# Fewer and larger DMAs, a third tile for f, and a newly searched order in an attention and FFN kernel

## The chip, the cores and the metric

The kernel runs on one core of one Trainium2 chip. The metric is the device time of one execution in microseconds (us), the median over runs; lower is better. The core has TensorE (PE in the profile, with its weight loads PEld), VectorE (DVE), ScalarE (ACT), GpSimd (POOL) and SyncE (SP), which here issues every DMA.

## The reference

Attention over 4 batches, 8 heads, 576 positions of 64 elements, with a retrieval from a memory mixed in by a gate; its output, laid out as 2304 tokens of 512, goes through a feed-forward network (FFN) of width 2048. Cut to what is computed:

```python
scores = scale * q @ k.T                      # causal: -1e9 above the diagonal
a = exp(scores - scores.max(-1)); a /= a.sum(-1) + 1e-9
local = a @ v
phi = lambda x: where(x > 0, x, exp(x) - 1.0) + 1.0
mem_out = (phi(q) @ M_prev) / ((phi(q) @ z_prev) + 1e-6)
g = sigmoid(beta)                             # one per head
attn = g * mem_out + (1 - g) * local          # 4 x 8 x 576 x 64
x = attn.transpose(0, 2, 1, 3).reshape(2304, 512)
h = x @ w_in                                  # 512 x 2048
out = (h * tanh(softplus(h))) @ w_out         # 2048 x 512
```

The weights w_in and w_out come as 64-bit floating point numbers; the kernel reads them as pairs of 32-bit words.

## The kernel before, in words

**Attention** goes by 16 pairs of heads, p = 4 bb + c for batch bb and quarter c of d_model; the text counts them from pair 1 (p = 0). `pair(p)` loads `f` (q and k transposed, 576 KB in all, in two DMAs, in four for pair 1), `qn` (q by rows), `z` (the memory's normaliser, one DMA per pair, spread over the partitions) and `v`. Then come S, the scores into PSUM banks (`bank<-f`); on DVE the mask with the running maximum (`w<-bank,mask`); on ACT the exponential with its sum (`w<-w,mx`); on GpSimd mostly the division by the sum (`w<-w,rc`); T, transposes into banks (`bank<-ident,w`), which ACT and DVE copy to `at`; and V, the product with v and the memory (`bank<-at,v`). Its result x is split in two parts: ACT copies the rounded part to `xo` (`CAST xo<-bank`), DVE puts the rest in `xl`. Both parts go by DMA to DRAM (`xs`), and for the first 512 tokens straight to the FFN's tile `xg` as well.

**FFN.** The 2048 hidden units are 16 units of 128. The first KA = 4 units run while attention goes, in five blocks of up to 512 tokens (`early`): `slot_h` makes h (`bank<-xg,wt`, three matmuls for each of four quarters, since x and the weights each are in two parts), ACT applies the activation and `out_a` multiplies by w_out (`bank<-wt,xg`); `ob` takes the sums to DRAM. The first block (block 0) takes x from pairs 1 to 4. The other 12 units follow after attention, in two groups of six: for each group three blocks of 768 tokens (a *round* each), in which `factors` loads x from `xs` and forms seven factors, `products` makes a two-by-two block product with seven products in place of eight (`bank<-xT,wi`, 126 matmuls a round), and `outputs` multiplies by w_out (`bank<-wt,xg`, 108 matmuls a round).

**Weights.** `word` loads one unit's words into `raw` (512 KB) and turns them into 32-bit numbers in five steps: ACT scales the high words (`ca<-raw`), DVE takes the sign and joins it, ACT scales the low words (`cs<-raw`), POOL adds both (`ca<-ca,cs`). `halves` then splits the number in two parts in `wt` or, by `split7`, in `wi`. ACT must load another function table to go from the exponential to the FFN's activation and back.

**What sets the order.** `Plan` is a list scheduler that runs when the program is built. Every operation has an engine, an estimated length, a priority (smaller goes first) and the buffers that it holds; a buffer is a tile of a `Ring` of fixed size, and an operation may be placed only when its ring has a free tile. `pick` chooses for each engine the ready operation of the best priority, `place` books its time, `schedule` repeats this until all are placed. On the chip each engine executes its list in that order and waits where an operand is not there. A priority in attention is `T0[p] + OFF[step]`: T0 is a number for each pair, OFF one for each kind of step ('lf' the load of f, 'lv' of v, 'S' the scores, 'V', and so on); CV gives the priority of the early units' conversions, and the numbers FB, FS, XP and TB those of the FFN. For TensorE the rule in `pick` prefers attention when it is ready and changes between attention and FFN by DRAIN, AGE and STAY. TABLE is what a change of ACT's table counts. EA = 6 is the number of pairs whose `nrm` scalings and phi step go partly by ACT. A transfer is planned at 370 GB/s, one behind the other on one wire, with 1.4 us behind it:

```python
if o.eng == "SP":
    self.wire = max(self.wire, start + 0.9) + o.kb / 370.0
    done = self.wire + 1.4
```

The rings that matter here: f 2 tiles, z 2, v 2, `xo` 2, `xl` 1, `raw` 2, `ca` 3, `cs` 3, `ob` 4. The tiles of attention are in one pool that is given back ahead of the first operation of the tail (`tail_tiles`).

## Time and profile before

| what | value |
|---|---|
| median of three runs | 569.87 us (568.3 to 571.32) |
| profiled execution: its time | 567.94 us |
| profiled execution: its span | 566.1 us |
| TensorE busy | 532.8 us, 94% of the span |
| VectorE busy | 433.6 us, 77% |
| ScalarE busy | 343.3 us, 61% |
| GpSimd busy | 192.0 us, 34% |
| moved by DMA | 99.78 MB, mean 176 GB/s |
| mean granted TensorE clock | 0.979 |

The span is the time from the first to the last recorded instruction; the execution's time adds 1.84 us around it. Shares of the whole span are means over stages that have different limits, so the rows below go by stage: the busy time of each engine in a stretch, and the timelines, in which a bracket at the end of a row is the time that the engine was idle ahead of it and what it had waited for. Since every instruction goes through one helper (`Queue`), all rows have that helper's line, L260, and are told apart by the tiles: `bank<-f` is a score, `bank<-at,v` is V, `bank<-xg,wt` makes h. The page's groups of TensorE leave out the tail's difference between early and late units: `bank<-wt,xg` is used by both.

### The profile page before, as it was taken

What the parts mean: (1) busy time and instruction counts of PE and PEld (TensorE: products, weight loads), DVE (VectorE), ACT (ScalarE), POOL (GpSimd) and SP (SyncE); (2) the same over time, 40 slices, a digit from 0 to 9 for tenths busy, and PEclk for the clock granted to TensorE, in tenths of its full rate; (3) what the DMA queues carried; (4) which work ended last, traced back from release to release, by engine and by line L of the source; (5) the groups of instructions that cost most, each with busy time, mean ns of one, the idle gap of its engine ahead of it and who ended that gap; (6) DMA issues with size and microseconds to landing.
All of it is one profiled execution on the core that took longest, in us unless ns stands there. A gap on an engine that the chain in (4) does not pass through costs nothing.

```text
span 566.1 us, 10611 instructions
## 1 busy us (share of the span) xinstructions
PE 532.8 (94%) x3684; PEld 442.2 (78%) x3684; DVE 433.6 (77%) x1039; ACT 343.3 (61%) x812; POOL 192.0 (34%) x268
## 2 busy tenths in 40 slices
PE   5596969999999999999999999999999899999997
PEld 3474647777776777788988899899889788989985
DVE  5799886999977985269779959749969995773722
ACT  6799889997999976366577235137328631521510
POOL 2578664798693797001121500000012310000000
PEclk9788979999999999999999999999999999999999
DMA  7566754676657742796556555444475617624004
GB/s 243 172 232 229 242 182 149 207 219 214 221 177 218 242 117 65 237 337 199 185 191 239 178 175 168 129 150 156 142 227 167 222 38 223 185 68 157 0 7 143
DMA packets 60740, 99.78 MB, mean 176 GB/s; under 512 B 6928, under 2 KB 32016, under 8 KB 60688
## 3 DMA queue, kind: packets, MB, share of 16 engines
q1 hardware_dynamic: 60688, 99.12, 54.2%
q8 instruction: 29, 0.48, 0.4%
q14 instruction: 23, 0.19, 0.1%
HBM read 73.40 MB, written 23.59 MB: 171 GB/s over the span
## 4 chain that ended last, share of the span: by engine, by line
PE 57%; DVE 16%; DMA 12%; ACT 9%; issue 3%; SPq 2%; POOL 1%; ACTq 0%; DVEq 0%
PE bank L260 57%; DMA raw<-in_w_out_dram 4%; DVE w L260 4%; ACT w L260 2%; SPq L260 2%; DMA part<-ob 2%; DVE at L260 2%; ACT L260 1%; DVE ca L260 1%; DMA f<-in_f_src_dram 1%; DMA qn<-in_qn_dram 1%; DVE xt L260 1%; DMA ob<-part 1%; DMA raw<-in_w_in_dram 1%; DVE wt L260 1%
## 5 line engine op out<-in xcount | busy, mean ns | idle before, releaser
L260 PE MATMUL bank<-wt,xg 128*128 128x512 f32 x864 | 200.9, 391 | 2.4 <-ACT wt L260 1.8
L260 PEld LDWEIGHTS bank<-wt,xg 128*128 128x128 f32 x864 | 161.2, 188 | 37.8 <-ACT wt L260 2.1
L260 PE MATMUL bank<-xT,wi 128*128 128x384 f32 x756 | 134.1, 335 | 1.9 <-DVE xg L260 1.1
L260 PEld LDWEIGHTS bank<-xT,wi 128*128 128x128 f32 x756 | 131.3, 188 | 3.8 <-DVE xg L260 2.1
L260 POOL TENSOR_TENSOR ca<-ca,cs 128x512 int32<-128x512 int32 x32 | 50.7, 1592 | 200.2 <-ACT cs L260 200.2
L260 ACT ACTIVATE w<-w,mx 128x576 f32<-128x576 f32 (+4 forms) x160 | 88.4, 558 | 9.4 <-DVE mx L260 9.1
L260 POOL TENSOR_SCALAR w<-w,rc 128x192 f32<-128x192 f32 (+4 forms) x148 | 85.4, 597 | 11.4 <-DVE rc L260 7.1
L260 ACT ACTIVATE bank<-bank 128x384 f32<-128x384 f32 (+2 forms) x92 | 45.2, 495 | 64.8 <-DVE bank L260 54.6
L260 DVE CUSTOM_DVE_ANT_0 w<-bank,mask 128x288 f32<-128x288 f32 (+4 forms) x160 | 60.3, 423 | 14.2 <-PE bank L260 14.2
L260 PE MATMUL bank<-f 64*128 64x288 f32 (+4 forms) x384 | 60.2, 442 | 10.4 <-DMA f<-in_f_src_dram 10.0
L260 PE MATMUL bank<-at,v 128*64 128x256 f32 (+2 forms) x512 | 57.4, 378 | 4.6 <-ACT at L260 3.7
L260 PE MATMUL bank<-xg,wt 128*128 128x512 f32 (+1 forms) x240 | 55.6, 382 | 6.1 <-DMA xg<-xl 2.7
L260 PEld LDWEIGHTS bank<-f 64*128 64x128 f32 x384 | 39.7, 204 | 26.4 <-issue 14.8
L260 DVE TENSOR_TENSOR xg<-bank,xg 128x384 fp32r<-128x384 f32 (+2 forms) x92 | 50.5, 567 | 12.0 <-ACT xg L260 11.8
L260 PEld LDWEIGHTS bank<-at,v 128*64 128x64 f32 x512 | 37.4, 143 | 25.1 <-ACT at L260 5.9
L260 PEld LDWEIGHTS bank<-xg,wt 128*128 128x128 f32 x240 | 41.5, 191 | 16.4 <-DMA xg<-xl 3.3
L260 DVE TENSOR_TENSOR ob<-bank,ob 128x512 f32<-128x512 f32 x36 | 24.4, 686 | 38.6 <-PE bank L260 36.3
L260 ACT CAST xg<-bank 128x384 fp32r<-128x384 f32 (+2 forms) x92 | 44.2, 501 | 0.9
L260 DVE COPY at<-bank 128x448 f32<-128x448 f32 x64 | 39.0, 646 | 5.3 <-PE bank L260 5.2
L260 PEld LDWEIGHTS bank<-ident,w 64*128 64x128 f32 x928 | 34.1, 142 | 10.2 <-issue 7.3
L260 DVE TENSOR_TENSOR bank<-u,bank 128x384 f32<-128x384 f32 x72 | 38.2, 556 | 3.7 <-PE bank L260 3.5
L260 PE MATMUL bank<-ident,w 64*128 64x64 f32 x928 | 37.1, 228 | 4.1 <-DVE ca L260 1.9
(53 smaller groups left out, 552.1 us busy)
## 6 DMA issues: line engine op xcount, KB each, us to landing
part<-ob SPq DMA_DIRECT2D x36, 256.0 KB, 3.1
xT<-xs SPq DMA_DIRECT2D x24, 384.0 KB, 6.3
ob<-part SPq DMA_DIRECT2D x36, 256.0 KB, 3.4
f<-in_f_src_dram SPq DMA_DIRECT2D x30, 288.0 KB, 4.5
raw<-in_w_in_dram SPq DMA_DIRECT2D x16, 512.0 KB, 5.0
raw<-in_w_out_dram SPq DMA_DIRECT2D x16, 512.0 KB, 4.4
qn<-in_qn_dram SPq DMA_DIRECT2D x16, 320.0 KB, 4.6
v<-in_vn_dram SPq DMA_DIRECT2D x16, 320.0 KB, 3.4
```

Source lines behind the costliest of these rows:

```text
L260: ins = f(*a, **kw)
```

## The change

- **DMAs.** f of a pair comes in one DMA instead of two (pair 1 keeps four). z comes for four pairs at once, into one tile `zall` that all pairs read; its ring is gone. The two parts of x lie side by side in one tile `xo` of [128, 2S], and leave in one DMA each to `xs` and, for the first 512 tokens, to `xg`. The tail's x factors are loaded per quarter with both parts in one, where it was per part with both quarters. The program has 306 DMAs in place of 361.
- **The planner's count of DMAs.** `place` keeps the planned ends of all transfers, and a DMA is planned no earlier than the end of the eighth one back (LANES = 8).
- **Rings.** f has three tiles. While attention runs, `ca` has one tile (was three), `cs` two (three), `ob` three (four); when attention's pool is given back, MORE adds `ca` 2, `cs` 1 and `ob` 1.
- **Numbers of the order.** T0, OFF, CV, DRAIN, AGE, STAY, TABLE (6 to 25.5), FS (20 to 8.7) have other values, and the tail's priorities have values of their own in TP. EA is 5. The planner's lengths of TensorE's operations grow by 0.05 to 0.06, and up to 90 us (COLD) they count 1.16 fold (before: 1.2 fold up to the first FFN matmul).

The core of the diff:

```diff
-EA = 6
+EA = 5
-CV = (21.0, 34.0, 41.0, 48.0)
-T0 = tuple(10.0 * p for p in range(16))
+CV = (32.0, 37.5, 46.3, 57.5)
+T0 = (0.0, 8.0, 25.7, 28.8, 41.7, 50.6, 62.1, 80.5, 89.4, 103.7, 106.9, 113.6, 118.4, 128.0, 130.0, 143.1)
...
-SLOTS = {"f": 2, "qn": 2, "phe": 1, "z": 2, "v": 2, "w": 6, "at": 6, "xo": 2, "xl": 1, "mx": 4, "sm": 2, "den": 3,
-         "rc": 2, "ob": 4, "raw": 2, "ca": 3, "cs": 3}
-KEPT = ("ob", "raw", "ca", "cs")
+SLOTS = {"f": 3, "qn": 2, "phe": 1, "v": 2, "w": 6, "at": 6, "xo": 2, "mx": 4, "sm": 2, "den": 3, "rc": 2}
+KEPT = {"raw": 2, "ca": 1, "cs": 2, "ob": 3}
+MORE = {"ca": 2, "cs": 1, "ob": 1}
+LANES = 8
...
         if o.eng == "SP":
             self.wire = max(self.wire, start + 0.9) + o.kb / 370.0
             done = self.wire + 1.4
+            self.landed.append(done)
+            self.lane = self.landed[-LANES] if len(self.landed) >= LANES else 0.0
...
-            s = max(now, o.ready, t, self.port if o.port else 0.0)
+            s = max(now, o.ready, t, self.port if o.port else 0.0, self.lane if eng == "SP" else 0.0)
...
-        chunks = [(0, 288), (S + 448, 2 * S), (288, S), (S, S + 448)] if p == 0 else [(0, S), (S, 2 * S)]
+        chunks = [(0, 288), (S + 448, 2 * S), (288, S), (S, S + 448)] if p == 0 else [(0, 2 * S)]
...
-        P.op("SP", 0.4, lambda: sy.dma_start(out=at(zb), in_=zz[:, 2 * p:2 * p + 2, :].rearrange("a b c -> a (b c)").to_broadcast([128, 2 * D])),
-             t0 + OFF['lq'] + 1.0, w=[k("z")], bufs=[zb], kb=64)
+        if c == 0:
+            z0 = slice(2 * D * p, 2 * D * p + 8 * D)
+            P.op("SP", 0.4, lambda: sy.dma_start(out=zall[:, z0], in_=zz[:, 2 * p:2 * p + 8, :].rearrange("a b c -> a (b c)").to_broadcast([128, 8 * D])),
+                 t0 + OFF['lz'], w=[("z", bb)], kb=400)
...
-        P.op("SP", 0.4, lambda: sy.dma_start(out=xs[bb][:, 0, c, :], in_=at(xob)), t0 + 5, r=[k("xo", 0), k("xo", 1)], w=[("xs", bb, c, 0)], bufs=[xob], kb=288)
-        P.op("SP", 0.4, lambda: sy.dma_start(out=xs[bb][:, 1, c, :], in_=at(xlb)), t0 + 5, r=[k("xl", 0), k("xl", 1)], w=[("xs", bb, c, 1)], bufs=[xlb], kb=288)
+        P.op("SP", 0.4, lambda: sy.dma_start(out=xs[bb][:, :, c, :], in_=at(xb2).rearrange("p (i t) -> p i t", i=2)), t0 + 5,
+             r=done, w=[("xs", bb, c, i) for i in range(2)], bufs=[xb2], kb=576)
...
-            split7(q, TB - 20 + 300 * gi + 5 * q)
+            split7(q, TB + TP['wi'] + TP['gap'] * gi + 5 * q)
```

What the numbers do to the order is seen in the lists of instructions themselves. SP at the program's start, before:

```order
L260 DMA f_101<-in_f_src_dram 128x288
L260 DMA f_101<-in_f_src_dram 128x128
L260 DMA f_101<-in_f_src_dram 128x288
L260 DMA f_101<-in_f_src_dram 128x448
L260 DMA f_102<-in_f_src_dram 128x576 x2
L260 DMA qn_103<-in_qn_dram 128x640
L260 DMA z_106<-in_zz_dram 128x128
L260 DMA qn_104<-in_qn_dram 128x640
L260 DMA z_107<-in_zz_dram 128x128
L260 DMA gt<-in_beta_dram 128x8
L260 DMA v_108<-in_vn_dram 128x640
L260 DMA v_109<-in_vn_dram 128x640
```

and after:

```order
L272 DMA v_104<-in_vn_dram 128x640
L272 DMA f_98<-in_f_src_dram 128x288
L272 DMA f_98<-in_f_src_dram 128x128
L272 DMA f_98<-in_f_src_dram 128x288
L272 DMA f_98<-in_f_src_dram 128x448
L272 DMA v_105<-in_vn_dram 128x640
L272 DMA f_99<-in_f_src_dram 128x1152
L272 DMA qn_101<-in_qn_dram 128x640
L272 DMA zall<-in_zz_dram 128x512
L272 DMA gt<-in_beta_dram 128x8
L272 DMA qn_102<-in_qn_dram 128x640
L272 DMA f_100<-in_f_src_dram 128x1152
```

v of pairs 1 and 2 now stand ahead of their f, z comes once, and f of pair 3 (`f_100`) is the twelfth DMA.

TensorE from the end of pair 4's V on, before (`xg` is x of block 0, `wt_81` and `wt_82` the first two units' w_in, `f_101` the scores of a later pair):

```order
L260 MATMUL bank_70<-at_120,v_109 64x128
L260 MATMUL bank_73<-xg,wt_82 128x512 x9
L260 MATMUL bank_74<-f_101 128x288
L260 MATMUL bank_75<-f_101 128x288
L260 MATMUL bank_70<-f_101 128x288
L260 MATMUL bank_71<-f_101 128x288
L260 MATMUL bank_76<-xg,wt_81 128x512 x3
L260 MATMUL bank_72<-f_101 128x448
L260 MATMUL bank_77<-f_101 128x448
L260 MATMUL bank_72<-f_101 128x64
L260 MATMUL bank_77<-f_101 128x64
L260 MATMUL bank_74<-f_101 128x320
```

and after, from the middle of the scores of pair 7 on, which follow pair 4's V:

```order
L272 MATMUL bank_76<-f_98 128x448
L272 MATMUL bank_73<-f_98 128x64
L272 MATMUL bank_76<-f_98 128x64
L272 MATMUL bank_70<-f_98 128x320
L272 MATMUL bank_72<-f_98 128x320
L272 MATMUL bank_70<-f_98 128x192
L272 MATMUL bank_72<-f_98 128x192
L272 MATMUL bank_74<-xg,wt_81 128x512 x9
L272 MATMUL bank_77<-xg,wt_82 128x512 x12
L272 MATMUL bank_73<-ident,w_108 128x64
L272 MATMUL bank_71<-ident,w_108 128x64
L272 MATMUL bank_73<-ident,w_108 128x64
```

Before, FFN matmuls stood straight behind V and between the scores; now three stand ahead of V, and 21 behind all scores of the next pair.

SP ahead of the second group's second round, before (`raw` from w_out are the group's last converted weights, `xT` the factors of x):

```order
L260 DMA raw_90<-in_w_out_dram 128x1024
L260 DMA raw_91<-in_w_out_dram 128x1024
L260 DMA xT_3030<-xs_65 128x2x384 x2
L260 DMA xT_3034<-xs_65 128x2x384 x2
L260 DMA xT_3035<-xs_66 128x2x384
L260 DMA raw_90<-in_w_out_dram 128x1024
L260 DMA xT_3035<-xs_66 128x2x384
L260 DMA raw_91<-in_w_out_dram 128x1024
```

and after:

```order
L272 DMA raw_87<-in_w_out_dram 128x1024
L272 DMA raw_86<-in_w_out_dram 128x1024
L272 DMA xT_2856<-xs_65 128x2x384 x2
L272 DMA xT_2860<-xs_65 128x2x384 x2
L272 DMA xT_2861<-xs_66 128x2x384 x2
L272 DMA raw_87<-in_w_out_dram 128x1024
L272 DMA out_dram<-ob_93 128x512
```

The group's fourth and fifth load of w_out now stand ahead of the factors; the sixth stays behind them.

## Rows read from the trace of the kernel before

**Rows 1.** Busy times by stage: stretch, length, busy (instructions), clock, DMA share, GB/s.

```profile
0.00:32.40 32.40, 20.33 (x166) 14.69 (x168) 22.70 (x94) 22.88 (x66) 14.24 (x28) 0.84 0.55 183
32.40:72.70 40.30, 32.48 (x355) 23.40 (x352) 37.81 (x111) 35.24 (x100) 28.40 (x40) 0.92 0.73 248
72.70:199.50 126.80, 121.43 (x1191) 88.64 (x1191) 110.19 (x362) 117.54 (x307) 90.56 (x142) 0.97 0.64 204
99.60:199.50 99.90, 98.96 (x1034) 73.22 (x1032) 89.31 (x301) 93.62 (x256) 74.19 (x120) 1.00 0.68 213
199.50:234.00 34.50, 34.50 (x364) 26.18 (x361) 23.06 (x67) 22.75 (x58) 22.43 (x40) 1.00 0.40 122
440.80:491.30 50.50, 47.59 (x235) 41.95 (x235) 39.08 (x64) 20.77 (x41) 5.77 (x3) 1.00 0.49 152
```

**Rows 2.** Timeline, 0 to 40 us: start, length, engine, operation [idle before <- releaser].

```profile
3.37 8.31 PE L260 MATMUL bank<-f 64*128 64x288 f32 x48 [3.37 <-DMA f<-in_f_src_dram]
...
18.29 4.49 PE L260 MATMUL bank<-f 64*128 64x288 f32 x24 [6.61 <-DMA f<-in_f_src_dram]
...
19.62 0.46 DVE L260 CUSTOM_DVE_ANT_0 w<-bank,mask 128x288 f32<-128x288 f32 x1 [2.65 <-PE bank L260]
...
23.20 1.08 ACT L260 COPY at<-bank 128x384 f32<-128x384 f32 x2 [2.96 <-PE bank L260]
```

**Rows 3.** Busy times by short stretches, same columns, first and middle of attention.

```profile
2.00:3.00 1.00, 0.00 (x0) 0.00 (x0) 0.00 (x0) 0.06 (x1) 0.24 (x1) 1.00 0.73 203
3.00:4.00 1.00, 0.63 (x3) 0.54 (x4) 0.00 (x0) 0.00 (x0) 0.00 (x0) 1.00 0.92 247
...
15.00:20.00 5.00, 1.71 (x8) 1.41 (x10) 2.28 (x15) 4.86 (x15) 4.54 (x9) 0.50 0.62 228
80.00:85.00 5.00, 5.00 (x19) 2.79 (x18) 3.50 (x18) 3.28 (x6) 5.00 (x10) 0.50 0.11 43
```

**Rows 4.** Timeline of TensorE, 40 to 85 us.

```profile
42.22 2.21 PE L260 MATMUL bank<-f 64*128 64x288 f32 x16
...
66.76 3.35 PE L260 MATMUL bank<-at,v 128*64 128x320 f32 x32
71.78 2.33 PE L260 MATMUL bank<-xg,wt 128*128 128x512 f32 x9 [1.67 <-DVE ca L260]
...
77.08 0.50 PE L260 MATMUL bank<-xg,wt 128*128 128x512 f32 x1 [1.68 <-DMA xg<-xo]
79.41 1.22 PE L260 MATMUL bank<-xg,wt 128*128 128x512 f32 x2 [1.83 <-DMA xg<-xl]
80.56 4.00 PE L260 MATMUL bank<-f 64*128 64x448 f32 x16
```

**Rows 5.** Timeline of ACT at the copy out of pair 13.

```profile
199.14 0.37 ACT L260 CAST xo<-bank 128x256 fp32r<-128x256 f32 x1 [0.54 <-PE bank L260]
```

**Rows 6.** Groups of ACT's instructions: count, busy us, mean ns, idle before.

```profile
L260 ACT ACTIVATE w<-w,mx 128x576 f32<-128x576 f32 (+4 forms) x160 | 88.4, 558 | 9.4 <-DVE mx L260 9.1
...
L260 ACT ACTIVATION_READ_ACCUMULATOR w<-w,mx 128x1 f32 x160 | 30.9, 193 | 0.0
L260 ACT ACTIVATE cs<-raw 128x512 int32<-128x512 uint32 x32 | 21.4, 676 | 12.3 <-DVE ca L260 12.3
```

**Rows 7.** Timeline of TensorE in the tail.

```profile
301.63 24.68 PE L260 MATMUL bank<-wt,xg 128*128 128x512 f32 x108
...
348.02 24.68 PE L260 MATMUL bank<-wt,xg 128*128 128x512 f32 x108
...
452.00 0.74 PE L260 MATMUL bank<-wt,xg 128*128 128x512 f32 x2 [1.79 <-ACT wt L260]
453.11 2.56 PE L260 MATMUL bank<-wt,xg 128*128 128x512 f32 x10 [0.37 <-DVE wt L260]
```

**Rows 8.** Timelines of SP and ACT around the late w_out load.

```profile
439.30 0.34 SPq L260 DMA_DIRECT2D raw<-in_w_out_dram  x1
...
446.64 0.69 ACT L260 ACTIVATE ca<-raw 128x512 f32<-128x512 f32 x1 [1.27 <-DMA raw<-in_w_out_dram]
```

More of the change, by code (lines that the diff above doesn't have):

```diff
@@ L48 @@
 SWITCH = 0.15
-DRAIN = 1.2
-AGE = 3.0
-STAY = 8.0
+COLD = 90.0
+DRAIN = 1.89
+AGE = 6.9
+STAY = 12.4
 def f32(ap):
@@ L135, in place @@
         o.start, o.end = start, start + o.dur
+        if o.tail and not self.grown:
+            self.grown = True
+            for name, n in MORE.items():
+                ring = self.rings[name]
+                ring.free += [(o.end, ring.size + k) for k in range(n)]
         done = o.end + LAT[o.eng]
@@ L238, in schedule @@
         return sorted(order, key=lambda o: (o.start, o.n))
-TABLE = 6.0
+TABLE = 25.5
 @with_exitstack
@@ L308, in attention_moe_kernel @@
     P.rings["wa"].moves = P.rings["wo"]
-    attp = None
-    for name, n in sorted(SLOTS.items(), key=lambda x: x[0] not in KEPT):
-        if name not in KEPT and attp is None:
-            attp = held.enter_context(tc.tile_pool(name="att", bufs=1))
+    for name, n in KEPT.items():
         P.rings[name] = Ring(name, n)
-        slot[name] = [(sb if name in KEPT else attp).tile(SHAPE[name], F32, name=f"{name}{k}") for k in range(n)]
+        slot[name] = [sb.tile(SHAPE[name], F32, name=f"{name}{k}") for k in range(n)]
+    attp = held.enter_context(tc.tile_pool(name="att", bufs=1))
+    zall = attp.tile([128, NP * 2 * D], F32, name="zall")
+    for name, n in SLOTS.items():
+        P.rings[name] = Ring(name, n)
+        slot[name] = [attp.tile(SHAPE[name], F32, name=f"{name}{k}") for k in range(n)]
     WA, WO7, WI7 = {}, {}, {}
@@ L325, in tail_tiles @@
             slot[name] = [pool.tile(shape, dt, name=f"{name}{k}") for k in range(LATE[name])]
+        for name, n in MORE.items():
+            slot[name] += [pool.tile(SHAPE[name], F32, name=f"{name}m{k}") for k in range(n)]
     def word(f, k, prio):
         src = (w_in, w_out)[k]
-        raw, a, s = P.buf("raw"), P.buf("ca"), P.buf("cs")
+        raw, a, s = (P.buf(n) for n in ("raw", "ca", "cs"))
         b = P.buf("bank", "conv") if f < KA else a
@@ L447, in mms @@
                     o += n
-            P.op("PE", sum(b - a for _, a, b in bank) / 600.0 + 0.02, mms, t0 + OFF['S'] + 0.1 * bi, r=need[bi],
+            P.op("PE", sum(b - a for _, a, b in bank) / 600.0 + 0.06, mms, t0 + OFF['S'] + 0.1 * bi, r=need[bi],
                  w=[k("s", bi, 0), k("s", bi, 1)], bufs=[fb, SM] + pb + W + MX, kind="S")
@@ L600, in hi @@
             def hi(q0=q0, nq=nq, pb=pb):
[L601 removed]
+                ac.copy(out=xo().bitcast(F32R)[:, q0:q0 + nq], in_=at(pb)[:, :nq])
             def lo(q0=q0, nq=nq, pb=pb):
[L604 to L607 removed]
+                ve.tensor_tensor(out=xl()[:, q0:q0 + nq], in0=at(pb)[:, :nq], in1=xo()[:, q0:q0 + nq], op=ALU.subtract)
@@ L608, in pair @@
+            P.op("ACT", nq / 1280.0 + 0.06, hi, t0 + OFF['hi'], r=[k("o", j)], w=[k("xo", j)], bufs=[pb, xb2])
+            P.op("DVE", nq / 960.0 + 0.07, lo, t0 + OFF['lo'], r=[k("o", j), k("xo", j)], w=[k("xl", j)], bufs=[pb, xb2])
+        done = [k(n, j) for n in ("xo", "xl") for j in range(2)]
         if p < NC:
             xb, n = P.buf("x"), BLOCKS[0][1]
-            for i, (src, sk) in enumerate(((xob, "xo"), (xlb, "xl"))):
-                P.op("SP", 0.4, lambda src=src, i=i: sy.dma_start(out=at(xb)[:, n * i:n * i + n], in_=at(src)[:, :n]), t0 + 5,
-                     r=[k(sk, 0), k(sk, 1)], w=[("x", 0, p, i, 0)], bufs=[src, xb], kb=256)
+            P.op("SP", 0.4, lambda: sy.dma_start(out=at(xb).rearrange("p (i t) -> p i t", i=2), in_=at(xb2).rearrange("p (i t) -> p i t", i=2)[:, :, :n]),
+                 t0 + 5, r=done, w=[("x", 0, p, i, 0) for i in range(2)], bufs=[xb2, xb], kb=512)
@@ L866, in attention_moe_kernel @@
             base = TB + 100 * (NB * gi + k)
-            X, got = factors(k, tag, base - 40)
+            X, got = factors(k, tag, base + TP['fac'])
             for i, q in enumerate(qs):
                 products(q, tag, X, got, base + 10 * i)
-            outputs(k, [KA + 2 * q + i for q in qs for i in range(2)], tag, base + 40, gi == 1)
+            outputs(k, [KA + 2 * q + i for q in qs for i in range(2)], tag, base + TP['out'], gi == 1)
     order = P.schedule()
```

75 lines of the change are left out of this document (37 added, 38 removed).

## The prediction

> **What bounds the kernel now.** I read four views. Pairs are counted from 1 (the first is p = 0 in the code). First the busy times by stage, with stage ends put where the trace shows an event: 32.4 us (pair 1 copied out), 72.7 (pair 4), 99.6 (pair 5), 199.5 (pair 13 [rows 5]), 234 (pair 16), and one late round, 440.8 to 491.3. The reader is to see who is full in which stage [rows 1]. Up to 32.4 us nobody is: ACT 22.88 of 32.40. From 32.4 to 72.7 DVE has 37.81 of 40.30 and ACT 35.24. From 72.7 to 199.5 ACT has 117.54 of 126.80, and TensorE joins it: from 99.6 on it is busy for 98.96 of 99.90. From 199.5 to 234 TensorE has 34.50 of 34.50, while ACT falls to 22.75. So ACT (with DVE close behind) sets when pair 13 is done, and from there the order of TensorE's own work sets the end: the span is the time of pair 13, plus the work TensorE has left, plus its waits in the last stage. I use that as the frame, since moving an FFN matmul from one side of the last pair to the other changes nothing on a TensorE that is full on both sides.
>
> Then the timelines, for the waits. At the start TensorE runs out at 11.7 us and waits 6.61 us for pair 3's f, which could be loaded only after pair 1 gave its tile back; DVE then idles 2.65 us and ACT 2.96 [rows 2]. Between 70 and 80 us TensorE, which takes its work in order, waits 1.67, 1.68 and 1.83 us in front of FFN matmuls of block 0, for a weight and for the two parts of x of pair 4 [rows 4]; the scores of a later pair are queued behind these 5.2 us. In the late stage TensorE waits 1.79 us for one converted w_out [rows 7]; a round of products and outputs takes 46.39 us from 301.63 to 348.02 and 50.50 in this stage [rows 1, 7], a loss of 4.1.
>
> **The change, part by part.** *Start.* The third f tile lets pair 3's f be asked for among the first loads. The 6.61 us do not all come back: the scores of pair 3 need banks that DVE frees only while it works through pair 2, so what can come back is DVE's 2.65 us and ACT's 2.96 [rows 2]. Against this, v of pair 1 (320 KB) now stands ahead of pair 1's f, and v of pair 2 ahead of f of pair 2. In these microseconds the queues moved 203 and 247 GB/s [rows 3], so 320 KB put about 1.3 to 1.6 us in front of the first score, which started at 3.37 [rows 2]; the second v is hidden, since DVE reaches pair 2 after its f has landed even so. 2.8, between the two, less 1.3 gives 1.5 us: **-1.5**, between -3.0 (v costs nothing) and +1.6 (ACT and DVE were held by something else).
>
> The Trainium skill would price that v lower: its page "DMA: Bandwidth & Descriptors", section "Anatomy of one DMA", fits a transfer as a fixed 2.0 us plus its bytes at 436 GB/s, which makes 0.75 us for 320 KB, an estimate by that page, and a sum better by about 0.6 us. The trace moved about half of that rate in these microseconds, and I keep the trace's.
>
> *Up to pair 13.* Counted along ACT's order up to pair 13's last copy out, the new order has seven more exponentials, one more of phi and one more copy of `at`, and leaves out two steps each of the first and second conversion activations, two output copies, one `qn` copy and two scalings (EA from 6 to 5 gives the last three to DVE and GpSimd). An exponential with its accumulator read is 0.558 + 0.193 us, a conversion step 0.676 [rows 6]: 7 x 0.75 = 5.3 more, 4 x 0.68 = 2.7 less. The others have no row here; at an estimated 0.5 us each, near the 0.558 of the exponential, two more and five less make 1.5 less. 5.3 - 2.7 - 1.5: **+1.1**. The number of table loads ahead of this point is the same (twelve besides the first).
>
> *Waits up to pair 13.* From 32.4 to 199.5 us ACT idles 5.1 + 9.3 = 14.3 us [rows 1]. In the new TensorE order the first block's FFN is no longer fed pair by pair: three matmuls stand behind pair 4's transposes, then its V and the whole scores of pair 7, and only then the other 21 of the first two units. The weight wait goes, since these scores give it their time. For x of pair 4 it is a matter of time: in the old order its second part had landed at 79.41 us, 9.3 us behind the end of pair 4's V (66.76 + 3.35) [rows 4]; the new order has a pair's scores and six matmuls in between, an estimated 3.3 + 1.4 = 4.7 us. So of the 5.2 us up to 4.6 could stay, or nothing where the copies and the transfer follow V at once. I take the middle, 2.3 left: **-3.0** (rounded). The bounds are -9 (most of ACT's idle time goes) and +3: the buffer `ca` has one tile in place of three while attention runs, so conversions go one at a time, and a late one would put a wait like the 1.67 us back, twice over.
>
> *The FFN work that moves.* Ahead of the end of pair 13's V, TensorE has 156 order rows of FFN in place of 180 and 188 rows of scores in place of 176. 24 FFN matmuls at 24.68 us / 108 = 0.229 us [rows 7] are 5.5 us that stay for later; 12 rows of scores, a pair, are an estimated 3.3 us done sooner (2.21 us for 16 of a pair's 24 instructions [rows 4]). **+2.2.** That 48 FFN matmuls in all move behind pair 16, with four gelus, their copies and a table load, is in this frame worth nothing more.
>
> *Late round.* In the old order the fourth w_out load of the second group stood behind the x factors of the next round: it was issued at 439.30 and landed 7.3 us later, where ACT waited for it [rows 8], and TensorE at 452.00 and 453.11 for its halves [rows 7]. The new order has the fourth and the fifth ahead of those factors, and TensorE's output matmuls of this round in one piece, with no products pushed between them. I take the whole 4.1 us: **-4.1**, with 0 as the other bound (the sixth load still stands behind the factors, and is first needed 48 matmuls, 11.0 us, into the round).
>
> *Costed at nothing.* 361 DMAs become 306, and an issue is 0.34 us of SP's time [rows 8]; SP waits for tiles most of the time, so its issue time is covered by that waiting, and it would cost that apiece only in the burst of loads behind pair 16. x's two parts in one transfer leave when the second is subtracted, about 0.5 us later than the first alone: covered, because their readers moved back by a pair. z for four pairs is read late in a pair. Eight transfers at a time is a number in the planner; on the chip it only reorders. `ob` has three tiles in place of four until the attention's tiles are gone: output copies could wait for a store, which is in the +3 above.
>
> **Sum.** -1.5 + 1.1 - 3.0 + 2.2 - 4.1 = -5.3 us. The profiled execution had a span of 566.1 us and a time of 567.94; against it the changed kernel comes to 560.8 and 562.6. That execution lies 1.9 us under the median of the three runs, 569.87; from the median the forecast is **564.5 us**.
>
> **Rivals.** *The waits change names.* ACT is nearly full, so a wait taken from TensorE becomes one for ACT or DVE, and half of the late gap stays because the sixth w_out is late: -1.5 + 1.1 + 0 + 2.2 - 2.0, about 569.7 us, no change. For it: ACT's 117.54 of 126.80; against it: it was less full, 35.24 of 40.30, where the waits are [rows 1].
>
> *TensorE starves and its clock falls: slower.* Up to pair 5 the order now holds 24 FFN matmuls in place of 48, so TensorE has more gaps between pairs 4 and 8. After its gap at the start the granted clock was 0.50 from 15 to 20 us, and 0.50 again from 80 to 85, behind the waits at 77 and 79 us [rows 3, 4], which is the 1.2 GHz level; 16 score instructions then took 4.00 us, and 2.21 at the full clock [rows 4]. At that level a pair's scores (3.3 us at the full clock, as above) and V (3.35 [rows 4]) need 2 x 6.65 = 13.3 us, and with the transposes more than the 40.30 / 3 = 13.4 us in which a pair went by between 32.4 and 72.7 [rows 1]: from there TensorE and not ACT sets the pace. At an estimated 5 us for each of two pairs they are 10 us on top of the sum, about 574.5. Against it: in the old order the same stretch had these gaps as well. The Trainium skill, page "TensorE: Matmul & The Clock Gate", Part 1, says that the throttled state is the default and activity releases it; by that rule an order that leaves TensorE idle pays twice, and the two rows at 0.50 agree with it.
>
> *More than I count.* If the searched order also takes most of ACT's 14.3 us (-9) and the start gives 3, the time is 569.9 - 3 + 1.1 - 9 + 2.2 - 4.1, about 557.
>
> *It doesn't do what it says.* If transfers on the chip do not keep to the planner's eight, loads land later than planned and engines wait in order for them; with the late gap unchanged that is -1.5 + 1.1 - 3 + 2.2, about 568.7, no change.
>
> **How the numbers follow.** Forecast 0.54, more than I count 0.10, waits change names 0.18, not as planned 0.06, starving 0.12. A measurement of this kernel can tell about 0.5%, 2.85 us, from no change, so 567.0 and 572.7 are the borders. The forecast's own range, with each term at its middle bounds, is 560 to 568; most of it, about 0.50 of the 0.54, is faster. Faster 0.60, same 0.28, slower 0.12. For 8 in 10 the range runs from 555 (a little under the better case) to 572 (the no-change cases, short of starving).
>
> **What would show it.** In the changed profile: the first score at about 4.7 us and no f wait at 11.7; scores of pair 3 before 18 us; pair 13's copy out at about 196 us, pair 16's near 222; ACT over 90% busy from 32 us to pair 13; the granted clock no lower than before in 50 to 90 us; one unbroken run of 108 output matmuls in the second group's first round, and 46.4 us from one round to the next. The forecast is wrong if pair 13 comes after 199 us, if windows at 0.50 grow, or if TensorE still waits for `wt` in that round.

## The result, and the profile after

The changed kernel takes 563.46 us (median of 4, 562.93 to 566.66) where the kernel before, beside it, took 570.6 us: a ratio of 0.9893, 95% interval 0.9844 to 0.9942. Timed again later it was 563.32 us, ratio 0.9869 (0.9829 to 0.9909). The profiled execution has a span of 561.3 us, 4.8 under the 566.1 of before. A caution for all that follows: the second profiled execution of the same changed program had a span of 567.5 us. One profile of this kernel gives the total to some 6 us only; what can be read from it is where waits stand, and totals come from the medians.

The busy times by stage, the stage ends again where a pair was copied out: 30.8 (pair 1), 67.1 (pair 4), 191.8 (pair 13) and 216.4 us (pair 16). Columns as in [rows 1]:

```profile
0.00:30.80 30.80, 21.79 (x166) 14.51 (x168) 21.24 (x93) 21.84 (x67) 13.39 (x28) 0.94 0.69 237
30.80:67.10 36.30, 29.27 (x352) 20.89 (x350) 35.51 (x117) 34.32 (x101) 28.89 (x43) 1.00 0.74 245
67.10:191.80 124.70, 120.53 (x1214) 90.14 (x1216) 115.29 (x383) 118.69 (x314) 98.35 (x153) 0.99 0.60 195
191.80:216.40 24.60, 24.60 (x296) 18.60 (x292) 13.37 (x32) 12.71 (x36) 14.08 (x26) 1.00 0.38 132
```

ACT has 21.84 + 34.32 + 118.69 = 174.85 us of work up to pair 13, 175.66 in [rows 1]; it idles 8.96 us in the first stage (9.52 before) and 7.99 in the next two (14.3 before). That is the whole of pair 13's 7.7 us (191.8 against 199.5): 0.6 less idle time at the start, 0.8 less work, 6.3 less idle time after it. TensorE is full from 191.8 to 216.4.

TensorE's timeline in attention, as [rows 2] and [rows 4]:

```profile
5.31 8.97 PE L272 MATMUL bank<-f 64*128 64x288 f32 x48 [5.31 <-DMA f<-in_f_src_dram]
14.79 2.32 PE L272 MATMUL bank<-f 64*128 64x288 f32 x10 [0.50 <-DMA f<-in_f_src_dram]
18.06 2.51 PE L272 MATMUL bank<-f 64*128 64x448 f32 x14 [0.95 <-DVE mx L272]
...
60.84 0.97 PE L272 MATMUL bank<-xg,wt 128*128 128x512 f32 x3 [1.87 <-DVE at L272]
61.73 3.35 PE L272 MATMUL bank<-at,v 128*64 128x320 f32 x32
...
70.01 5.05 PE L272 MATMUL bank<-xg,wt 128*128 128x512 f32 x21
...
77.45 0.86 PE L272 MATMUL bank<-ident,w 64*128 64x64 f32 x14 [1.31 <-DVE xg L272]
...
80.03 4.85 PE L272 MATMUL bank<-at,v 128*64 128x320 f32 x32
```

The first score starts at 5.31 us, 1.94 later than before. The 6.61 us for pair 3's f have become 0.50, and 0.95 for a bank. The 21 FFN matmuls at 70.01 wait for nothing, though they need x of pair 4 as well. What is late next is 1.31 us at 77.45, the transposes of a pair waiting for a bank whose last reader is the FFN's split of h on DVE; V at 80.03 then takes 4.85 us, where it takes 3.35 at the full clock (61.73). The clock of these stretches, columns as before:

```profile
75.00:80.00 5.00, 3.43 (x63) 2.52 (x62) 4.89 (x9) 4.65 (x11) 3.72 (x5) 0.97 0.64 216
80.00:85.00 5.00, 5.00 (x36) 3.08 (x36) 4.35 (x13) 4.79 (x9) 3.41 (x7) 0.69 0.01 3
```

TensorE behind pair 16, and in the late stage, as [rows 7]:

```profile
238.87 5.60 PE L272 MATMUL bank<-xg,wt 128*128 128x512 f32 x24
247.99 0.69 PE L272 MATMUL bank<-xT,wi 128*128 128x384 f32 x1 [3.53 <-ACT xT L272]
249.47 1.97 PE L272 MATMUL bank<-xT,wi 128*128 128x384 f32 x5 [0.79 <-DVE xT L272]
251.24 6.83 PE L272 MATMUL bank<-xg,wt 128*128 128x512 f32 x24
...
439.67 24.68 PE L272 MATMUL bank<-wt,xg 128*128 128x512 f32 x108
...
486.06 24.68 PE L272 MATMUL bank<-wt,xg 128*128 128x512 f32 x108
```

The outputs of the second group's first round are one row of 108, and from 439.67 to the next at 486.06 it is 46.39 us: the late round lost nothing in this execution. (In the second profile of the changed kernel it is whole too, but the round ahead of it takes 47.88 us, from 397.91 to 445.79, with 0.75 us of waiting for ACT.) But there is a wait that no row of before has: 3.53 and 0.79 us at 248 us, in front of the tail's second product, and behind it 24 matmuls in 6.83 us that took 5.60 at 238.87. The granted clock of 245 to 255 us fell with it:

```profile
245.00:250.00 5.00, 1.22 (x3) 0.82 (x4) 5.00 (x7) 4.05 (x8) 0.00 (x0) 0.69 0.18 66
250.00:255.00 5.00, 5.00 (x17) 4.22 (x16) 4.48 (x8) 1.93 (x4) 1.28 (x1) 0.62 0.24 79
```

### The profile page after: what moved, and what is told of

Read it like the earlier page. It is cut to its first block, busy times and chain, and to the rows that moved or that the text cites. A ratio compares the mean times of both kernels' runs of the same rounds, so it can differ in the third digit from the quotient of the medians.

```text
span 561.3 us, 10520 instructions
## 1 busy us (share of the span) xinstructions
PE 532.4 (95%) x3684; PEld 444.4 (79%) x3684; DVE 430.6 (77%) x1040; ACT 340.7 (61%) x809; POOL 193.0 (34%) x270
## 4 chain that ended last, share of the span: by engine, by line
PE 64%; DVE 14%; ACT 9%; DMA 8%; POOL 2%; issue 2%; SPq 0%; DVEq 0%; ACTq 0%
PE bank L272 64%; DVE w L272 4%; DMA raw<-in_w_in_dram 3%; DVE at L272 2%; ACT w L272 2%; POOL cam L272 2%; DMA raw<-in_w_out_dram 2%; ACT L272 1%; ACT xg L272 1%; ACT bank L272 1%; DVE den L272 1%; DMA xg<-xs 1%; ACT at L272 1%; DMA qn<-in_qn_dram 1%; DVE wt L272 1%
## 5 line engine op out<-in xcount | busy, mean ns | idle before, releaser
L272 PE MATMUL bank<-xg,wt 128*128 128x512 f32 (+1 forms) x240 | 53.4, 378 | 2.0 <-DVE at L272 1.9
L272 POOL TENSOR_TENSOR cam<-cam,cs 128x512 int32<-128x512 int32 x9 | 19.0, 2111 | 80.2 <-ACT cs L272 62.1
L272 DVE TENSOR_TENSOR ob<-bank,ob 128x512 f32<-128x512 f32 x27 | 18.3, 689 | 29.3 <-PE bank L272 24.3
L272 DVE TENSOR_TENSOR xt<-xt,xt 128x768 f32<-128x768 f32 x30 | 28.7, 972 | 15.1 <-DMA xt<-xs 12.7
```

The costliest lines, as they stand in the source:

```text
L272: ins = f(*a, **kw)
```

## The experiments

Three kinds: one thing moved on a queue of the changed kernel or the old one, with all other orders as they were; one part undone; and the numbers of the order exchanged between the two kernels. Of each diff the core is shown; lines that only carry names along are left out. To compare kernels that do a different amount of FFN work beside attention, I split each profiled span in two: the *attention part* is the time at which pair 16 was copied out, less 0.2285 us (24.68 / 108, [rows 7]) for each FFN matmul that stands in TensorE's order ahead of pair 16's V, and the *rest* is the remaining span. This takes each of these matmuls at TensorE's price alone, and it is one execution per kernel. How far executions differ is seen from five profiles with the changed kernel's order up to pair 16 (its own two, e1_xt_ahead, e9_xt_and_conv and, but for the split DMAs, e4_split_dmas): 170.4 to 174.5. All ratios are to the kernel before, run beside them.

| kernel | ratio, 95% interval | pair 16 out | FFN matmuls ahead | attention part | rest |
|---|---|---|---|---|---|
| before | | 234.0 | 240 | 179.2 | 386.9 |
| after | 0.9893, 0.9844 to 0.9942 | 216.4 | 192 | 172.5 | 388.8 |
| after, second time (e13_after_again) | 0.9869, 0.9829 to 0.9909 | 217.5 | 192 | 173.6 | 393.9 |
| e1_xt_ahead | 0.9923, 0.9898 to 0.9948 | 216.8 | 192 | 172.9 | 390.9 |
| e2_v_behind | 0.9926, 0.9892 to 0.9961 | 217.3 | 192 | 173.4 | 389.1 |
| e4_split_dmas | 0.9887, 0.9855 to 0.9918 | 218.4 | 192 | 174.5 | 391.3 |
| e9_xt_and_conv | 0.9859, 0.9820 to 0.9897 | 214.3 | 192 | 170.4 | 387.0 |
| e12_xt_conv_v | 0.9848, 0.9807 to 0.9889 | 215.8 | 192 | 171.9 | 388.2 |
| e7_f_two | 0.9922, 0.9891 to 0.9954 | 225.9 | 228 | 173.8 | 392.4 |
| e5_old_numbers | 1.0001, 0.9976 to 1.0027 | 224.7 | 228 | 172.6 | 392.0 |
| e8_before_new_numbers | 1.0040, 1.0006 to 1.0074 | 232.8 | 228 | 180.7 | 387.6 |
| e11_before_numbers_f3 | 1.0006, 0.9967 to 1.0044 | 234.4 | 228 | 182.3 | 389.8 |
| e10_before_tail_numbers | 0.9940, 0.9911 to 0.9969 | 232.6 | 240 | 177.8 | 384.6 |
| e3_before_wout_ahead | 0.9993, 0.9969 to 1.0016 | 234.7 | 240 | 179.8 | 386.8 |

**The late round: one load's place, or the whole row of conversions.** In the kernel before, after the order is planned:

```diff
     order = P.schedule()
+    wo = [o for o in order if o.eng == "SP" and o.w[0][0] == "c" and o.w[0][2] == 1 and o.w[0][1] >= 10][4]
+    fac = [o for o in order[:order.index(wo)] if o.eng == "SP" and o.w[0][:2] == (("t", 1, 1), "x") and o.w[0][2] != "12"]
+    for o in fac:
+        order.remove(o)
+    order[order.index(wo) + 1:order.index(wo) + 1] = fac
```

> The kernel before with one edit to SP's order: the fifth w_out load of the second group stands ahead of the five xT loads that preceded it. Theory of the prediction (place in the queue): it lands some 4 us sooner than at 446.6, TensorE's waits at 452.00 and 453.11 go, and the round takes 46.4 to 48 us instead of 50.50: 2.5 to 4.1 us faster than before. Rival (the tile of raw, not the queue: the load was issued at 439.30, right when the third load's words had been read at 439.28, and the sixth came at 447.92, when the fifth's had been read): the whole row of conversions is late, the wait moves to the sixth, and the gain is 0 to 1.5 us.

Ratio 0.9993: nothing. TensorE, and ACT's steps for the weight it waits for:

```profile
441.85 8.36 PE L261 MATMUL bank<-wt,xg 128*128 128x512 f32 x36
...
452.47 0.73 PE L261 MATMUL bank<-wt,xg 128*128 128x512 f32 x2 [1.19 <-ACT wt L261]
...
491.84 24.68 PE L261 MATMUL bank<-wt,xg 128*128 128x512 f32 x108
```

```profile
450.14 0.68 ACT L261 ACTIVATE cs<-raw 128x512 int32<-128x512 uint32 x1 [2.70 <-DVE ca L261]
...
451.80 0.61 ACT L261 CAST wt<-ca 128x512 fp32r<-128x512 f32 x1
```

The load no longer ends a wait of ACT. Instead a later conversion step (450.14) waits 2.70 us for DVE's step ahead of it, and the split that TensorE needs is at 451.80 and ends TensorE's wait at 452.47, where it was 452.00 [rows 7]. The round is 49.99 us. So the place behind the factors, on which the prediction put the term, was worth 0.5 us (and the load at 439.30 is the fifth of the group, not the fourth, as the prediction has it: the fourth stood ahead of the factors before too).

The rival, the whole row, was tried by giving the kernel before the tail's new priorities alone, those of the conversions (`wi`, `wo`, `gap`), of the factors (`fac`) and of the outputs (`out`). Of the diff, with the lines of the last two left out:

```diff
+TP = {'wi': -33.4, 'wo': -53.2, 'gap': 238.4, 'fac': -29.7, 'out': 63.6}
-            split7(q, TB - 20 + 300 * gi + 5 * q)
+            split7(q, TB + TP['wi'] + TP['gap'] * gi + 5 * q)
...
-                split(f, 1, TB - 15 + 300 * gi + 5 * q)
+                split(f, 1, TB + TP['wo'] + TP['gap'] * gi + 5 * q)
```

> The kernel before with the changed kernel's tail priorities alone; the order is the same up to about 390 us (the 1658th of TensorE's rows), so only the second group's conversions and factors move. In e3_before_wout_ahead the one load's place in the queue gave 0.5 us of the round's 4.1. Theory (the whole row of w_out conversions was planned too late, on ACT, DVE and SP together): the round from the second group's first outputs to its next ones takes 46.4 to 46.9 us in place of 50.50, 3.6 to 4.1 us faster than before. Rival (the loss is the factors' or the bandwidth's): 49 us or more.

Ratio 0.9940, 3.6 us of the 569.23 us beside it, and the round is whole:

```profile
439.84 24.68 PE L261 MATMUL bank<-wt,xg 128*128 128x512 f32 x108
...
486.23 24.68 PE L261 MATMUL bank<-wt,xg 128*128 128x512 f32 x108
```

439.84 to 486.23 is 46.39 us. That the tail's priorities give the late round's gain is shown. What they move is seen on SP: the group's first load of w_out goes out at 411.77 us in place of 419.47, its last at 438.76 in place of 447.92, and so the whole row of conversions is earlier. Since the priorities of the factors and outputs changed with them, that the conversions alone would do it is likely, not shown.

**v ahead of f.** The changed kernel with the two v loads behind the f of their pair:

```diff
     order = P.schedule()
+    for p in range(2):
+        v = next(o for o in order if o.w and o.w[0] == (p, "v"))
+        goal = [o for o in order if o.eng == "SP" and o.w[0][:2] == (p, "f")][-1]
+        order.remove(v)
+        order.insert(order.index(goal) + 1, v)
```

> The changed kernel with v of pair 1 behind pair 1's f and v of pair 2 behind pair 2's f on SP, all else in the same order. Theory (v ahead costs its transfer): the first score starts near 3.4 us instead of 5.31, pair 1's copy out comes at about 29 us instead of 30.8, and since ACT and DVE set the pace up to pair 13 the end moves by the same 1.3 to 1.9 us. Rival (the start is held by something else, since pair 2's copy out was no earlier in the changed kernel than before, 43.25 against 42.97): the first score moves, the end by less than 0.5 us.

```profile
3.40 9.15 PE L273 MATMUL bank<-f 64*128 64x288 f32 x48 [3.40 <-DMA f<-in_f_src_dram]
...
60.97 4.98 PE L273 MATMUL bank<-at,v 128*64 128x320 f32 x32
...
77.33 0.94 PE L273 MATMUL bank<-ident,w 64*128 64x64 f32 x14 [1.92 <-DVE xg L273]
...
80.57 5.42 PE L273 MATMUL bank<-at,v 128*64 128x320 f32 x32
```

The first score is at 3.40 us instead of 5.31, and pair 1 is out at 29.45 instead of 30.76. (The first score is at 3.40 in e12_xt_conv_v too, and at 4.64 to 5.31 in the four profiles with the changed kernel's start, so v's price there is 1.2 to 1.9 us. At pair 1's copy out these four lie between 28.83 and 31.40, the two without it at 29.45 and 30.06, and the price no longer shows.) By pair 5 the gain is gone: 86.40 against 85.30. The wait for the bank is 1.92 us instead of 1.31, V behind it takes 5.42 us instead of 4.85, and the clock of that stretch is 0.52 instead of 0.69:

```profile
80.00:85.00 5.00, 5.00 (x28) 2.62 (x26) 4.27 (x13) 3.92 (x8) 1.78 (x4) 0.52 0.00 0
```

No gain in the total, as the rival had it: the ratio, 0.9926, is above both of the changed kernel's, and the intervals overlap. e12_xt_conv_v has the same move on top of another and says the same, below.

**The number of DMAs.** The changed kernel, each of these transfers in two at the same place:

```diff
-sy.dma_start(out=F()[:, a:b], in_=fsrc[:, a:b])
+[sy.dma_start(out=F()[:, u:v], in_=fsrc[:, u:v]) for u, v in ([(0, S), (S, 2 * S)] if p else [(a, b)])]
...
-sy.dma_start(out=xs[bb][:, :, c, :], in_=at(xb2).rearrange("p (i t) -> p i t", i=2))
+[sy.dma_start(out=xs[bb][:, i, c, :], in_=at(xb2)[:, S * i:S * i + S]) for i in range(2)]
```

> The changed kernel with f of pairs 2 to 16 in two DMAs again and x's two parts in one DMA each again, each pair of DMAs at the place where the one stood; 35 DMAs more, nothing else moved. Theory (the number of DMAs is not what gave the time): within 0.5 us of the changed kernel. Rival (fewer, larger DMAs are the gain): 2 to 5 us slower, with f or x landing later in the rows of the first 220 us.

Ratio 0.9887, the changed kernel's. Joining these 35 pairs of transfers by itself gave nothing that can be measured; the other 20 of the 55 DMAs saved (z and the tail's loads) were not split again.

**Which half of the change gave the gain.** The numbers of the order (T0, OFF, CV, EA, DRAIN, AGE, STAY, TABLE, FS and the tail's) were exchanged: the new tiles, DMAs and planner with the old numbers, and the old ones with the new numbers.

> The changed kernel's DMAs, tiles and count of DMAs, planned with the numbers of the kernel before (T0, OFF, CV, EA, DRAIN, AGE, STAY, TABLE, FS and the tail's priorities). Theory (the order gave the time, the DMAs and tiles little): within 1.5 us of the kernel before, slower than the changed kernel by 4 us or more, with the late round's 50 us and a wait of some us behind pair 4 back. Rival (DMAs and tiles gave it): within 2 us of the changed kernel.

> The kernel before (two f tiles, its own DMAs and rings) planned with the numbers of the changed kernel. Theory (order): 3 to 6 us faster than the kernel before, with the late round at 46.4 us; what is missing against the changed kernel is the third f tile's share, about 1.5 us at the start. Rival (the numbers need the new tiles): no faster than before.

Neither has the gain: 1.0001 and 1.0040. The first is the total that the theory named, but not for its reason. By the table the attention part of e5_old_numbers is 172.6 us, as in the changed kernel, and what it gains there it loses again in the rest, 392.0 us. (Its profiled execution, 566.33 us, was the lowest of its twelve runs, so some of that gain may be luck; but the second profile of the changed kernel, 569.24 us and the highest of its seven, has 173.6.) e8_before_new_numbers is the other way round: a rest of 387.6 and an attention part of 180.7, above that of before. (e5_old_numbers and e8_before_new_numbers have the same 228 FFN matmuls ahead, so nothing need be taken off to compare them: pair 16 is out at 224.7 and 232.8.)

The traces also say where in the rest e5_old_numbers loses. From pair 16's copy out to the second round of outputs of the first group (348.02 before, 346.90 after, 348.37 and 354.01 in the two exchanges), less 0.2285 us for each FFN matmul fewer ahead of pair 16 than the 240 of before, it takes 114.0 us before, 119.6 after, 120.9 in e5_old_numbers and 118.5 in e8_before_new_numbers. So both exchanges lose 4 to 7 us in the stage behind pair 16, as the changed kernel does. The late round is 48.63 us in e5_old_numbers (441.14 to 489.77), 46.39 in e8_before_new_numbers (446.78 to 493.17).

Some of e8_before_new_numbers' waits in attention:

```profile
17.96 5.83 PE L262 MATMUL bank<-f 64*128 64x288 f32 x24 [4.72 <-DMA f<-in_f_src_dram]
...
48.90 0.79 PE L262 MATMUL bank<-xg,wt 128*128 128x512 f32 x1 [3.40 <-DMA xg<-xo]
...
75.21 4.43 PE L262 MATMUL bank<-xg,wt 128*128 128x512 f32 x17 [0.16 <-DMA xg<-xl]
...
83.59 0.78 PE L262 MATMUL bank<-ident,w 64*128 64x64 f32 x14 [2.88 <-DVE xg L262]
```

4.72 us for f, 3.40 for the first part of x of a pair, behind which TensorE's later work is queued, and 2.88 for a bank. (The new numbers do bring the new order of block 0's FFN matmuls: the row at 75.21 is the last 17 of 21 that stand behind a pair's whole scores, and waits 0.16 us.)

Then the third f tile, taken from the changed kernel and given to e8_before_new_numbers:

```diff
-SLOTS = {"f": 3, "qn": 2, "phe": 1, "v": 2, "w": 6, "at": 6, "xo": 2, "mx": 4, "sm": 2, "den": 3, "rc": 2}
+SLOTS = {"f": 2, "qn": 2, "phe": 1, "v": 2, "w": 6, "at": 6, "xo": 2, "mx": 4, "sm": 2, "den": 3, "rc": 2}
```

> The changed kernel with two tiles for f instead of three, planned anew with its own numbers. Theory (the new numbers pay only with the third f tile): the wait for pair 3's f is back with 4 to 7 us, pair 3 is copied out at 58 us or later instead of 54.86, and the kernel is 2 to 5 us slower than the changed one. Rival (another tile or the joined x makes the difference between e8_before_new_numbers and the changed kernel): within 1 us of the changed kernel.

> The kernel before with the new numbers, as e8_before_new_numbers, and a third tile for f; DMAs, x's two tiles and the rings of the conversions as before. Theory (the third f tile is what the numbers need): pair 3 copied out before 56 us, 4 to 7 us faster than e8_before_new_numbers, so 0.990 to 0.995 of the kernel before. Rival (the rest of the change is needed too): no more than 2 us faster than e8_before_new_numbers, no faster than before.

```profile
18.83 5.87 PE L272 MATMUL bank<-f 64*128 64x288 f32 x24 [4.85 <-DMA f<-in_f_src_dram]
```

Without the third tile the wait for f is back, 4.85 us at 18.83, and yet pair 3 is out at 52.94 us, sooner than the 54.86 of the changed kernel: the expectation failed there (the kernel was planned anew, so its order differs in more than f). The kernel loses some 2 us (565.79 against 563.32 beside it; the intervals overlap). With the third tile the old structure gains nothing over before (1.0006) and still waits 4.18 us for x:

```profile
48.14 0.80 PE L262 MATMUL bank<-xg,wt 128*128 128x512 f32 x1 [4.18 <-DMA xg<-xo]
```

So the attention part falls from 178 to 180 us in the kernels with the old planner, tiles and numbers, and 181 to 182 with the new numbers, to 170 to 175 in all that have the new planner and tiles, whichever numbers, whether f has two tiles or three and x goes in one DMA or two. What of the new structure does it (the count of eight transfers and the lengths of TensorE's work in the planner, x's two parts as one tile and one operation, the rings of `ca`, `cs` and `ob`) I didn't separate, and it stays open. What ACT waited for between pair 1's and pair 13's copy out narrows it down (us in all, times, longest), first before, then in e8_before_new_numbers:

```profile
ACT cs L260 <- DVE ca L260: 3.0, 3, 1.6
ACT bank L260 <- PE bank L260: 2.9, 1, 2.9
...
ACT cs L262 <- DVE ca L262: 2.8, 3, 1.1
ACT bank L262 <- PE bank L262: 2.7, 1, 2.7
```

The first is a conversion step that waits for the step ahead of it on DVE, the second the activation of an h that waits for TensorE. The five kernels with the old planner and tiles have both, 1.7 to 3.2 and 2.2 to 2.9 us; the nine profiles with the new ones, e5_old_numbers among them, have 0.4 to 1.0 us of the first and none of the second. So these waits go with the planner and tiles, whichever numbers.

**The wait behind pair 16.** SP's list in the changed kernel shows what stands ahead of the last loads for the tail's first factors (`xt`), and DVE's what waits for them:

```profile
225.69 2.80 SPq L272 DMA_DIRECT2D xt<-xs  x3
229.33 5.59 SPq L272 DMA_DIRECT2D xg<-xs  x8
234.97 1.55 SPq L272 DMA_DIRECT2D xt<-xs  x3
...
237.58 1.21 SPq L272 DMA_DIRECT2D xt<-xs  x2
239.05 0.33 SPq L272 DMA_DIRECT2D raw<-in_w_in_dram  x1
```

```profile
242.19 1.95 DVE L272 TENSOR_TENSOR xt<-xt,xt 128x768 f32<-128x768 f32 x2 [10.46 <-DMA xt<-xs]
```

Three of eight xt loads go out, then eight loads of `xg` in 5.59 us, then the other five. (The expectation below says that the xg loads first wait for a free tile of x; the trace shows 0.84 us between the third xt load and the first of them, and no such wait by name.) First, those five alone were moved ahead:

```diff
     order = P.schedule()
+    late = [o for o in order if o.eng == "SP" and o.w[0][:3] == (("t", 0, 0), "x", "12")]
+    goal = next(o for o in order[order.index(late[0]):] if o.eng == "SP" and o.w[0][0] == "x")
+    for o in late:
+        if order.index(o) > order.index(goal):
+            order.remove(o)
+            order.insert(order.index(goal), o)
```

> The changed kernel with one edit to SP's order alone: the five xt loads of the first tail round that stood behind the eight loads of xg now stand ahead of them; every other engine's order is as it was. Theory (queue place): DVE waited 10.46 us for xt and TensorE 3.53 + 0.79 us for the factors cut from it, and ran 24 matmuls behind that gap in 6.83 us instead of 5.5; all of this, some 5.7 us, comes from xt standing behind loads that first had to wait for a free tile of x. So 4 to 5.7 us faster than the changed kernel, about 558 to 559 us in its runs' terms, 0.98 of the kernel before. Rival (bandwidth): the queues moved 300 GB/s and more in these microseconds, so what xt gains xg loses, and TensorE waits for xg instead: 0 to 1 us faster.

No gain: 0.9923. DVE's timeline shows where it went:

```profile
235.20 1.95 DVE L273 TENSOR_TENSOR xt<-xt,xt 128x768 f32<-128x768 f32 x2 [3.05 <-DMA xt<-xs]
244.50 0.43 DVE L273 TENSOR_SCALAR cs<-raw 128x512 int32<-128x512 int32 x1 [7.34 <-DMA raw<-in_w_in_dram]
```

xt is added up at 235.20 instead of 242.19, but the next instruction on DVE is a weight's conversion, and it waits 7.34 us for its words, whose load stands behind all the others here; the factors stand behind it. The rival named the queues, and they were full or nearly so: from 225 to 245 us of the changed kernel their busy share was 0.86 to 1.04 at 221 to 366 GB/s, and in e1_xt_ahead TensorE waits 0.92 us for xg at 242.71, which it did not in the changed kernel. So the conversion steps were moved too:

```diff
+    conv = [o for o in order[beg:end + 1] if o.eng in ("DVE", "ACT", "POOL") and o.w[0][:3] in raws]
+    last_cut = order[end]
+    for o in conv:
+        order.remove(o)
+    order[order.index(last_cut) + 1:order.index(last_cut) + 1] = conv
```

Here `beg` to `end` runs from the first sum of xt to the last factor cut from it, and `raws` are the weights whose loads stand behind the xt loads.

> The changed kernel with the xt loads ahead of the xg loads, as in e1_xt_ahead, and with the conversion steps of two weights on ACT and DVE (two on each) moved behind the last factor cut from these xt. In e1_xt_ahead xt came at 235.2 instead of 242.2 us, but the next instruction on DVE, a conversion, waited 7.34 us for its words, and the factors behind it. Theory (DVE and ACT take their instructions in order, and a conversion whose words come last stands ahead of the factors): now the waits of TensorE at 244 to 251 us and the half clock behind them go, 4 to 6 us faster than the changed kernel, span 555 to 557. Rival: the conversions are then late for the next products and the waits come back there, or TensorE waits for xg: under 1.5 us.

```profile
239.91 0.94 PE L273 MATMUL bank<-xg,wt 128*128 128x512 f32 x3 [1.60 <-DMA xg<-xs]
241.35 3.67 PE L273 MATMUL bank<-xg,wt 128*128 128x512 f32 x15 [0.51 <-DMA xg<-xs]
244.85 1.23 PE L273 MATMUL bank<-xT,wi 128*128 128x384 f32 x6
245.92 5.64 PE L273 MATMUL bank<-xg,wt 128*128 128x512 f32 x24
```

```profile
245.00:250.00 5.00, 5.00 (x25) 4.30 (x24) 3.68 (x6) 3.63 (x6) 1.29 (x1) 1.00 0.25 92
250.00:255.00 5.00, 5.00 (x26) 4.47 (x26) 4.89 (x9) 3.38 (x6) 1.29 (x1) 1.00 0.59 170
```

The product waits for nothing, the 24 matmuls behind it take 5.64 us, and the clock is 1.00. What is left are 1.60 + 0.51 us for xg: here the rival of e1_xt_ahead has its part. The stretch from pair 16's copy out to the first unbroken row of 108 outputs is 126.8 us (214.28 to 341.07), and 128.2 in e12_xt_conv_v (215.82 to 344.04), which has the same move; in the four profiles with the changed kernel's order there it is 130.5 (216.36 to 346.90) to 134.0. Two exchanged rows on one engine gave nothing; the same move on all three engines that work on the factors gave 2 to 7 us in this stretch. The total moved by less than the 4 to 6 us expected: 0.9859 is 0.6 to 1.9 us under the changed kernel's two ratios. The span of 557.4 owes 2.1 us to an attention part that the edit doesn't touch.

Last, this with v behind f as well:

> e9_xt_and_conv with v of pairs 1 and 2 behind their f as well, as in e2_v_behind. Theory (by e2_v_behind's trace the start's 1.3 us were used up by pair 5, in a longer stretch at half clock and a longer wait for a bank): within 1 us of e9_xt_and_conv. Rival (the start's gain comes through when nothing follows that takes it): 1 to 2 us faster than e9_xt_and_conv.

Ratio 0.9848, e9_xt_and_conv's 0.9859: the same. The changed kernel itself ran beside it:

> The changed kernel unchanged, on the chip of these runs, so that the others have it beside them: 0.985 to 0.994 of the kernel before, as measured first, and its profile shows which waits come again: the one for the factors at 245 to 251 us surely, the granted clock of single stretches of the first 100 us not to the digit.

```profile
249.82 0.69 PE L272 MATMUL bank<-xT,wi 128*128 128x384 f32 x1 [4.20 <-ACT xT L272]
251.30 1.97 PE L272 MATMUL bank<-xT,wi 128*128 128x384 f32 x5 [0.79 <-DVE xT L272]
```

The wait behind pair 16 is there again, 4.20 + 0.79 us. By ratios e9_xt_and_conv and e12_xt_conv_v are 0.6 to 2.6 us under the changed kernel's two; both are clearly faster than the kernel before, but the intervals overlap with the changed kernel's, so that they beat it in the total too is likely and not shown.

## Why the prediction was right, step by step

The total was right (564.5 forecast, 563.46 measured; span 560.8 forecast, 561.3 measured), and in part that is luck: the terms up to pair 13 missed by 4.3 us together (-7.7 for -3.4), and a stage that had no price cost 4.8 us, in the opposite direction.

- **Start, -1.5.** Right in sign, its size not shown. Pair 1 is out 1.6 us sooner, but ACT idles only 0.6 less in the first stage, and the other 1.0 is ACT's work that no longer stands ahead of this point (21.84 us against 22.88); pair 2 is out at 43.25 us, no sooner than the 42.97 of before. v's price is 1.2 to 1.9 us at the first score, where the queues' rates gave 1.3 to 1.6. The Trainium skill's fit ("DMA: Bandwidth & Descriptors", "Anatomy of one DMA", 0.75 us as an estimate by that page) was further off; that section gives it for DMAs that GpSimd issues, and here SP issues them. e2_v_behind shows that this price is gone by pair 5, and e7_f_two that the third tile isn't what makes pair 3 early.
- **ACT's work up to pair 13, +1.1.** It was -0.8 (174.85 against 175.66 us), a miss of 1.9. The counts came out as forecast, 153 exponentials in place of 146, and the lengths of all instructions add up to 2.4 us more (219.2 against 216.8). But records that follow each other at once overlap, and the busy time counts the overlap once; so a sum of lengths is not ACT's time.
- **Waits up to pair 13, -3.0.** This step failed: ACT's idle time after pair 1's copy out fell by 6.3 us. I took the 5.2 us that TensorE showed at FFN matmuls of block 0 as the measure and left 2.3 of them for x of pair 4. These waits went altogether (70.01 waits for nothing): x of pair 4 went out in one DMA 2.9 us behind its V (67.95 us), where the second part had gone out 4.5 us behind it (74.60). But they were the wrong measure. e8_before_new_numbers has the FFN matmuls in the new order and hardly waits there (0.16 us), and its ACT idles 15.1 us in the same stretch, more than the 14.3 of before. Of the 6.3 us, 5.0 are ACT's own waits for the conversion step on DVE (3.0 to 0.9) and for h (2.9 to none), which go with the new planner and tiles; which part of those is open. That ACT was 95% busy from pair 1 to pair 13 (153.0 of 161.0 us), which the prediction had named as a sign (over 90%), says little: before it was 91% (152.8 of 167.1).
- **FFN work that moves, +2.2.** From pair 13's to pair 16's copy out it is 24.5 us in place of 34.5; the count of matmuls and scores gave 25.7.
- **Late round, -4.1.** Right in size (46.39 us a round; e10_before_tail_numbers 3.6 us), wrong in its cause: the queue's place gave 0.5 us, the tail's priorities together the rest.
- **Costed at nothing.** This failed. The prediction named the burst of loads behind pair 16 as the place where SP could cost time, and gave it no price. With -7.7 up to pair 13, +2.2 and -4.1, the sum would be -9.6; the span fell by 4.8. The other 4.8 us are at 245 to 257 us: 3.53 + 0.79 of waiting and 1.2 of the lower clock (6.83 - 5.60), 5.5 in all, a little more than is missing (and the six products between took 0.69 + 1.97 us, 1.23 in e9_xt_and_conv). The xt loads had become eight of 96 KB in place of four, five of them behind eight xg loads on queues that were nearly full, with conversions ahead of the factors on DVE and ACT.
- **The clock.** "TensorE starves" did not come: the granted clock of 75 to 85 us was 0.97 and 0.69, where [rows 3] has 0.50 from 80 to 85, and from 30.8 to 67.1 us it was 1.00, 0.92 in [rows 1]. It fell instead behind the wait at 248, to 0.62. That agrees with the Trainium skill, "TensorE: Matmul & The Clock Gate", Part 1 (throttled is the default, activity releases it): in e9_xt_and_conv, where the gap is gone, the clock stays at 1.00.

## What to carry to other kernels

When a sum of steps comes out right, check the steps: here -7.7 stood for -3.4 and an unpriced +4.8 made it good. A load that lands too late in a list-scheduled kernel has followers on several engines; moving it alone hands the wait to the next instruction in order, so move the consumer's whole row, and price the transition between stages, where loads for both stages meet, as a stage of its own. Numbers searched for one set of tiles and one planner gave nothing as a whole on another (1.0040), though the tail's alone did (0.9940), and the better tiles nothing in the total with the old numbers (1.0001): such parts have to be judged together, and stage by stage.
